# Order of TensorE's work in an attention round: value products, scores and both heads' transposes in one stretch, then the up products

## The chip, the cores and the metric

One core of one Trainium2 chip runs the kernel. The metric is the device time of one execution, in microseconds (us). A core has five engines with a queue of instructions each, executed in order: TensorE (PE in the profile; its weight loads are the row PEld), VectorE (DVE), ScalarE (ACT), GpSimd (POOL) and SyncE (SP), which here only issues DMAs. TensorE writes to PSUM, of which there are eight banks of 512 fp32 columns; ScalarE and VectorE read them.

## The reference

The kernel computes three parts one after the other (shortened; B=2, H=8, S=576, D=64; 1152 tokens, width 512, hidden width 1536):

```python
# 1: attention with a memory term, causal
a = softmax(mask(q @ k.T / 8))              # per batch and head
local = a @ v
q_p = where(q > 0, q, exp(q) - 1) + 1
mem = (q_p @ M_prev) / (q_p . z_prev + 1e-6)
x = g * mem + (1 - g) * local               # g = sigmoid(beta), heads side by side: [1152, 512]
# 2: gated MLP
gt, val = x @ w_gate, x @ w_val             # the "up" products
x = (gt * sigmoid(gt) * val) @ w_out
# 3: top-1 mixture of 8 experts with a capacity
e = argmax(x @ w_gate2); x = prob[e] * (relu(x[kept] @ w1[e]) @ w2[e])
```

## The kernel before, in words

All products are fp32 in effect. The up products split each operand into a high and a low part (xh, xl; wh, wl) and add three products, so that TensorE can take them in its faster fp32 form; scores, transposes and value products are plain fp32.

**Attention** is cut into 40 units. A group is a batch b, a half e of the sequence (rows 0 to 255, or 256 to 575) and a pair p of heads; it has two or three units, one for each block of up to 128 query rows. `first[n]` is the first unit of group n. For a unit u these functions emit the work:

- `emit_s` (L195): the scores of both heads into one PSUM tile `s` (two buffers), and the mask. `emit_max` (L215): VectorE's negated row maxima, scaled. `emit_exp` (L224): ScalarE's exponential from `s` into `P`, with row sums; two instructions, one a head, or one for the short last block.
- `emit_norm` (L230): VectorE adds 1e-9 to the sums and inverts them, GpSimd scales `P`.
- `emit_t(u, x)` (L238): transposes of head x of `P` on TensorE into a PSUM bank `tp`, and a copy to `PT`, which in all units is ScalarE's.
- `emit_av` (L264): value products from `PT` into the PSUM tile `u` (one buffer). In a group's last unit it adds the memory term, and ScalarE and VectorE write the group's result as `xh` (L287) and `xl` (L288). The next group's first value products need `u` back, so they wait for `xl`.

**The phi chores** prepare q_p for the memory term, for each batch and each of five row blocks: `phi_load`, `phi_exp` (ScalarE), `phi_sum` (VectorE, then GpSimd), `phi_norm` (VectorE, then GpSimd's division, L157 to L162), `phi_t` (L164: four transposes into a PSUM bank `tphi`, and ScalarE's copy to `ph`). They and the loads are laid on **ticks** by a table of constants `T` (L299 to L316): `at_tick(t, ...)` puts a chore on tick t, `do(t)` runs tick t's chores.

**The order** is written out by hand: the whole kernel stands under a manual schedule, so each engine executes its instructions in the order in which the Python code emits them. The generator `attn` (L318) runs rounds k = -3 to 40 of three ticks each. In round k the scores of unit k+3 are computed (LA = 3), the normalization of unit k+2 and the exponential of k+3, the transposes of k and the value products of k-1. After each tick it yields, and the driving loop (L537) may then take a **piece** from the generator `up` (L428): six up products, half of one result in a PSUM bank `gv`. Two pieces fill a bank. With the first piece of a bank `up` emits the evaluation of the bank before (tanh on ScalarE, L459, and VectorE's products L460 and L465), and with every piece a share of the preparation of the next weights: ScalarE's copies wh (L405), VectorE's or GpSimd's differences wl (L408), VectorE's unpacking of the raw weights (L374 to L379), and loads and stores of weights. The number of pieces by a tick is `cnt * total // (tb - ta)`: none before tick 35 (round 11), then 28 pieces up to tick 65 and 68 from there to the end, so three or four a round.

`gv`, `tp` and `tphi` share three PSUM banks (L83). A bank is given out again when all that reads it is done.

After attention, `up(2)` (L623) does the second batch's up products with the preparation of w_out; then come the down products with the routing, and the experts.

Of the kernel before, what the change touches and what calls it, by code (L numbers as in the profile page):

```python
# [36 lines left out]
T = dict(LA=3, lv0=-7, lv1=-21, le=-21, sc=-17, lp=-2, sk0=0, sk1=1, sq0=-5, sl0=-2, sq1=-6, sl1=-4, pl=-20,  # L37
         pe=0, ps=2, pn=4, pt=9, k00=-3, k01=-1, k02=1, k03=4, k04=8, kb0=-2, kb1=-4, kb2=4, kb3=2,
         kb4=8, lb=-11, n0=2, ns=9, RW=3, RS=2, ev0=1, ev1=1, ev2=1, lo0=8, lo1=24, sp0=-9, ka=8,
         kb=2, kc=0, w0=-15, w1=-3, rb=1, ob=2, vb=5, qb=5, Pb=4, xb=4, kk=0, xf=7, sx=2, t00=5, t01=1,  # L40
         t02=5, t03=8, t04=0, tb0=3, tb1=0, tb2=4, tb3=-1, tb4=-1, pre=1, rk=[8, 10], gt=[6, 7, 10,
         11], xr=7)
# [3 lines left out]
def tile_attention_moe(  # L46
# [36 lines left out]
    def bank(name):  # L83
        return psb.tile([128, 512], F32, tag="m", bufs=3, name=name)
# [12 lines left out]
    def cols(n):  # L97

        e = groups[n][1]
        return (HALF, S - HALF, S) if e else (0, HALF, HALF)  # L100
# [79 lines left out]
    NU = len(units)  # L180
# [14 lines left out]
    def emit_s(u):  # L195
        n, i = units[u]
        o, m = QT[i]
        w = o + m
        s = psa.tile([128, 2, 512], F32, tag="s", bufs=2, name="s")
        s_t[u] = s  # L200
        heads = [op_t[n][64 * h:64 * h + 64] for h in range(2)]
        if i < 4:
            for h, t in enumerate(heads):
                nc.tensor.matmul(s[:, h, 0:w], lhsT=t[:, 0, o:w], rhs=t[:, 1, 0:w], start=True, stop=False)  # L204
            for h in range(2):
                nc.tensor.matmul(s[:, h, o:w], lhsT=identb, rhs=maskb, start=False, stop=True)  # L206
        else:
            c = S // 2
            for a in range(2):
                for h, t in enumerate(heads):  # L210
                    nc.tensor.matmul(s[64 * h:64 * h + 64, a, 0:c], lhsT=t[:, 0, o:w], rhs=t[:, 1, a * c:a * c + c],
                                     start=True, stop=(a == 0), skip_group_check=True)
            nc.tensor.matmul(s[:, 1, c - 64:c], lhsT=identb, rhs=maskb2, start=False, stop=True, skip_group_check=True)

    def emit_max(u):  # L215
        P = at.tile([128, 2, 512], F32, tag="P", bufs=T["Pb"], name="P")
        st = at.tile([128, 3, 2], F32, tag="st", bufs=5, name="st")
        sv, vs = views(u, s_t[u], P)
        k = len(vs)
        nc.vector.tensor_reduce(out=st[:, 0, 0:k], in_=sv, axis=AX.X if k == 2 else AX.XY, op=ALU.max, negate=True)  # L220
        nc.vector.tensor_scalar(st[:, 0, 0:k], st[:, 0, 0:k], 0.125, None, op0=ALU.mult)  # L221
        p_t[u] = (P, st, vs)

    def emit_exp(u):  # L224
        P, st, vs = p_t[u]
        for x, (a, c, gm) in enumerate(vs):
            nc.scalar.activation(c, a, AF.Exp, bias=st[:, 0, x:x + 1], scale=0.125, accum_out=st[:, 1, x:x + 1])  # L227
        s_t.pop(u)

    def emit_norm(u):  # L230
        P, st, vs = p_t[u]
        k = len(vs)
        nc.vector.tensor_scalar(st[:, 1, 0:k], st[:, 1, 0:k], 1e-9, None, op0=ALU.add)
        nc.vector.reciprocal(st[:, 2, 0:k], st[:, 1, 0:k])  # L234
        for x, (a, c, gm) in enumerate(vs):
            nc.gpsimd.tensor_scalar(c, c, st[:, 2, x:x + 1], gm, op0=ALU.mult, op1=ALU.mult)  # L236

    def emit_t(u, x):  # L238

        n, i = units[u]  # L240
        P = p_t[u][0]
        if x == 0:
            pt_t[u] = at.tile([128, 2, 512], F32, tag="PT", bufs=2, name="PT")
        PT = pt_t[u]
        t = bank("tp")
        mode = T["ev" + str(0 if u < first[NP] else 1 if u < first[2 * NP] else 2)]
        ev = (nc.scalar.copy, nc.vector.tensor_copy)[(x % 2, 0, 1, x % 2 * (u % 2))[mode]]
        tv = t.rearrange("p (j m) -> p j m", m=128)
        if i < 4:
            for j in range(i + 1):  # L250
                nc.tensor.transpose(out=tv[:, j, :], in_=P[:, x, j * 128:(j + 1) * 128], identity=ident)  # L251
            ev(PT[:, x, 0:128 * (i + 1)], t[:, 0:128 * (i + 1)])  # L252
        else:
            pf, ptf = (z.rearrange("p a b -> p (a b)") for z in (P, PT))
            for y, j in enumerate(((0, 1, 2), (3, 4))[x]):
                kw = QT[j][1]
                nc.tensor.transpose(out=tv[0:kw, y, :], in_=pf[:, j * 128:j * 128 + kw], identity=ident)
            if x == 0:
                ev(ptf[:, 0:384], t[:, 0:384])
            else:  # L260
                ev(ptf[:, 384:512], t[:, 0:128])
                ev(ptf[0:64, 512:640], t[0:64, 128:256])

    def emit_av(u):  # L264
        n, i = units[u]
        vt = v_t[n]
        o, m = QT[i]
        PT = pt_t.pop(u)
        p_t.pop(u)
        ptf = PT.rearrange("p a b -> p (a b)")  # L270
        g0, gw, _ = cols(n)
        if u == first[n]:
            u_t[n] = psb.tile([128, 512], F32, tag="u", bufs=1, name="u")
        U = u_t[n]
        c0 = o - g0
        for j in range(i + 1):
            kw = QT[j][1]
            for h in range(2):
                rhs = PT[:, h, j * m:j * m + m] if i < 4 else ptf[0:kw, j * 128 + 64 * h:j * 128 + 64 * h + 64]
                nc.tensor.matmul(U[64 * h:64 * h + 64, c0:c0 + m], lhsT=vt[0:kw, j, 64 * h:64 * h + 64],  # L280
                                 rhs=rhs, start=(j == 0 and u == first[n]), stop=False, skip_group_check=True)
        if u + 1 == NU or units[u + 1][0] != n:
            b, e, p = groups[n]
            zt, mt, ph = batch_t[b]
            U, gs = u_t.pop(n)[:, 0:gw], slice(g0, g0 + gw)
            nc.tensor.matmul(U, lhsT=mt[:, p, :], rhs=ph[e][:, p, :], start=False, stop=True, skip_group_check=True)
            nc.scalar.copy(xh[b][:, p, gs], U)  # L287
            nc.vector.tensor_sub(xl[b][:, p, gs], U, xh[b][:, p, gs].bitcast(F32))  # L288
# [3 lines left out]
    def at_tick(t, fn, *args):  # L292
        chores.setdefault(t, []).append((fn, args))

    def do(t):
        for fn, args in chores.pop(t, ()):
            fn(*args)

    for n, (b, e, p) in enumerate(groups):  # L299
        k = 3 * (first[n] - LA)  # L300
# [4 lines left out]
    for b in range(B):  # L305
        k = first[2 * NP * b]
        for i in range(5):
            t = 3 * (k + T["k%s%d" % ("0b"[b], i)])
            if b or i > 1:
                at_tick(t + T["pl"], phi_load, b, i)  # L310
            at_tick(t + T["pe"], phi_exp, b, i)
            at_tick(t + T["ps"], phi_sum, b, i)
            at_tick(t + T["pn"], phi_norm, b, i)
            at_tick(t + T["pt"] + T["t%s%d" % ("0b"[b], i)], phi_t, b, i)
        if b:
            at_tick(3 * k + T["lb"], load_batch, b)  # L316

    def attn():  # L318
        for t in range(min(chores), -3 * LA):
            do(t)  # L320
        for k in range(-LA, NU + 1):
            do(3 * k)
            if k + LA < NU:
                emit_s(k + LA)
                emit_max(k + LA)
            if 0 <= k < NU:
                emit_t(k, 0)
            yield 3 * k
            do(3 * k + 1)
            if 0 <= k + LA - 1 < NU:  # L330
                emit_norm(k + LA - 1)
            if k + LA < NU:
                emit_exp(k + LA)
            if 0 <= k < NU:
                emit_t(k, 1)
            yield 3 * k + 1
            do(3 * k + 2)
            if 0 <= k - 1:
                emit_av(k - 1)
            yield 3 * k + 2  # L340


# [194 lines left out]
    for t in attn():  # L537
        if t < t0:
            continue
        if gi == 0 and t >= t1:  # L540
            for _ in gens[0][0]:
                pass
            gi, cnt, done = 1, 0, 0
        cnt += 1
        gen, ta, tb, total = gens[gi]
        while done < cnt * total // (tb - ta):
            next(gen, None)
            done += 1
# [613 lines left out]
```

## Time and profile before

| | |
|---|---|
| time, median of 3 runs | 562.18 us (559.9 to 564.96) |
| profiled execution | 562.79 us, span 561.0 us |
| mean granted TensorE clock | 0.983 |
| busy: PE, PEld, DVE, ACT, POOL | 94%, 77%, 66%, 49%, 38% of the span |
| attention and first up products | from the start to about 225 us |
| second batch's up products | about 225 to 305 us |

The busy shares are averages over stages with different limits. A busy TensorE is not TensorE at its peak: products are pipelined, so the distance from start to start is a better measure of their cost than the duration of one. Rows of a timeline give start, duration, engine, line, operation, operands and count, and in brackets the idle time of the engine just before it and what ended it. PEclk is the granted clock as a share of full speed; a stretch without a record of it is shown as 1.00.

### The profile page before, as it was taken

What the parts mean: (1) busy time and instruction counts of PE and PEld (TensorE: products, weight loads), DVE (VectorE), ACT (ScalarE), POOL (GpSimd) and SP (SyncE); (2) the same over time, 40 slices, a digit from 0 to 9 for tenths busy, and PEclk for the clock granted to TensorE, in tenths of its full rate; (3) what the DMA queues carried; (4) which work ended last, traced back from release to release, by engine and by line L of the source; (5) the groups of instructions that cost most, each with busy time, mean ns of one, the idle gap of its engine ahead of it and who ended that gap; (6) DMA issues with size and microseconds to landing.
All of it is one profiled execution on the core that took longest, in us unless ns stands there. A gap on an engine that the chain in (4) does not pass through costs nothing. (4 is left out here: it accounts for less than half of the span.)

```text
span 561.0 us, 9629 instructions
## 1 busy us (share of the span) xinstructions
PE 525.5 (94%) x3433; PEld 431.2 (77%) x3433; DVE 370.3 (66%) x788; ACT 272.3 (49%) x603; POOL 213.8 (38%) x259
## 2 busy tenths in 40 slices
PE   4789997999989999999999999999978999999996
PEld 2446776887767789999999887778766978888774
DVE  6778888557786541678877487975867681728080
ACT  4467665466644452233353234434767562726171
POOL 4767647547264331222223475863223111020220
PEclk9998998899989999999999999998999999999999
DMA  8568384326552110599981335354789855464430
GB/s 274 199 218 255 107 288 136 95 69 256 172 142 84 39 39 1 175 271 277 275 263 32 120 87 215 94 184 161 245 299 305 294 201 186 132 240 158 168 105 8
DMA packets 43005, 96.33 MB, mean 172 GB/s; under 512 B 4598, under 2 KB 15350, under 8 KB 41408
## 3 DMA queue, kind: packets, MB, share of 16 engines
q1 hardware_dynamic: 41184, 91.04, 50.3%
q0 software_dynamic: 1760, 4.50, 2.1%
q8 instruction: 36, 0.59, 0.4%
q14 instruction: 25, 0.20, 0.1%
HBM read 78.68 MB, written 17.72 MB: 172 GB/s over the span
## 5 line engine op out<-in xcount | busy, mean ns | idle before, releaser
L444 PE MATMUL gv<-xh,wh 128*128 128x256 f32 (+1 forms) x384 | 123.2, 321 | 4.1 <-ACT PT L252 1.9
L444 PE MATMUL gv<-xh,wl 128*128 128x256 f32 (+1 forms) x384 | 114.7, 299 | 1.2 <-POOL wl L408 1.1
L444 PE MATMUL gv<-xl,wh 128*128 128x256 f32 (+1 forms) x384 | 114.0, 297 | 0.0
L236 POOL TENSOR_SCALAR P<-P,st,omg 128x128 f32<-128x128 f32 (+4 forms) x72 | 65.3, 915 | 66.7 <-DVE st L234 38.5
L444 PEld LDWEIGHTS gv<-xh,wh 128*128 128x128 f32 x384 | 73.3, 191 | 8.9 <-issue 3.6
L444 PEld LDWEIGHTS gv<-xh,wl 128*128 128x128 f32 x384 | 73.3, 191 | 2.2 <-POOL wl L408 2.1
L444 PEld LDWEIGHTS gv<-xl,wh 128*128 128x128 f32 x384 | 73.5, 191 | 0.7
L1030 POOL DMA_INDIRECT out_dram<-hT,gi x13 | 15.6, 1197 | 124.5 <-ACT hT L1029 101.7
L408 POOL TENSOR_TENSOR wl<-wf,wh 128x512 fp32r<-128x512 f32 x27 | 39.7, 1471 | 59.6 <-ACT wh L405 56.0
L227 ACT ACTIVATE P<-s,st 128x128 f32<-128x128 f32 (+4 forms) x72 | 39.1, 549 | 31.9 <-DVE st L221 22.7
L220 DVE TENSOR_REDUCE st<-s 128x2 f32<-128x256 f32 (+4 forms) x40 | 32.2, 805 | 21.4 <-PE s L206 17.0
L818 PE MATMUL y<-wo_h,hh 128*128 128x512 f32 x108 | 43.3, 401 | 0.0
L252 ACT COPY PT<-tp 128x128 f32<-128x128 f32 (+3 forms) x64 | 27.2, 426 | 33.0 <-PE tp L251 32.9
L679 DVE SCALAR_TENSOR_TENSOR prod<-y,wrb 128x512 f32<-128x512 f32 x56 | 34.8, 686 | 11.9 <-ACT xr L676 11.9
L818 PE MATMUL y<-wo_h,hl 128*128 128x512 f32 x108 | 42.4, 392 | 0.0
L818 PE MATMUL y<-wo_l,hh 128*128 128x512 f32 x108 | 42.4, 392 | 0.0
L405 ACT CAST wh<-wf 128x512 fp32r<-128x512 f32 x54 | 33.7, 624 | 14.3 <-DMA wf<-wsp 14.3
L460 DVE SCALAR_TENSOR_TENSOR th<-th,gv 128x256 f32<-128x256 f32 (+1 forms) x48 | 21.6, 451 | 27.0 <-ACT th L459 26.9
L280 PE MATMUL u<-PT,vt 128*64 128x128 f32 (+1 forms) x480 | 34.7, 279 | 4.1 <-DVE xl L288 4.1
L204 PE MATMUL s<-qk 64*128 64x128 f32 (+3 forms) x128 | 30.1, 553 | 6.8 <-DMA qk<-in_qk_dram 4.1
L1010 DVE SCALAR_TENSOR_TENSOR hcl<-w,hch 128x288 fp32r<-128x288 f32 x24 | 10.9, 456 | 35.1 <-ACT hch L1009 35.0
L280 PEld LDWEIGHTS u<-PT,vt 128*64 128x64 f32 x480 | 24.4, 143 | 12.1 <-issue 4.9
(372 smaller groups left out, 1250.2 us busy)
## 6 DMA issues: line engine op xcount, KB each, us to landing
hT<-in_w_dram SPq DMA_DIRECT2D x64, 512.0 KB, 5.4
wr<-in_wgv_dram SPq DMA_DIRECT2D x12, 1024.0 KB, 5.9
wf<-wsp SPq DMA_DIRECT2D x15, 512.0 KB, 5.0
wor<-in_w_out_dram SPq DMA_DIRECT2D x12, 512.0 KB, 4.6
wsp<-wf SPq DMA_DIRECT2D x10, 512.0 KB, 6.8
disp<-pad SPq DMA_DIRECT2D x16, 257.0 KB, 7.0
xd<-disp SPq DMA_DIRECT2D x14, 257.0 KB, 7.3
qk<-in_qk_dram SPq DMA_DIRECT2D x8, 320.0 KB, 4.2
```

What stands on the lines that cost most here:

```text
L204: nc.tensor.matmul(s[:, h, 0:w], lhsT=t[:, 0, o:w], rhs=t[:, 1, 0:w], start=True, stop=False)
L220: nc.vector.tensor_reduce(out=st[:, 0, 0:k], in_=sv, axis=AX.X if k == 2 else AX.XY, op=ALU.max, negate=True)
L227: nc.scalar.activation(c, a, AF.Exp, bias=st[:, 0, x:x + 1], scale=0.125, accum_out=st[:, 1, x:x + 1])
L236: nc.gpsimd.tensor_scalar(c, c, st[:, 2, x:x + 1], gm, op0=ALU.mult, op1=ALU.mult)
L252: ev(PT[:, x, 0:128 * (i + 1)], t[:, 0:128 * (i + 1)])
L280: nc.tensor.matmul(U[64 * h:64 * h + 64, c0:c0 + m], lhsT=vt[0:kw, j, 64 * h:64 * h + 64], rhs=rhs, start=(j == 0 and u == first[n]), stop ...
L405: nc.scalar.copy(hi[:, sl], w[:, sl])
L408: (nc.gpsimd if pool_ else nc.vector).tensor_sub(lo[:, sl], w[:, sl], hi[:, sl].bitcast(F32))
L444: nc.tensor.matmul(a, lhsT=wt[:, s, c, :], rhs=xt[b][:, c, sl], start=(c == 0 and y == 0), stop=(c == KC - 1 and y == 2))
L460: nc.vector.scalar_tensor_tensor(out=th[:, 0:w], in0=th[:, 0:w], scalar=1.0, in1=a, op0=ALU.add, op1=ALU.mult)
L679: nc.vector.scalar_tensor_tensor(out=prod[e % 2], in0=y, scalar=1.0, in1=wrb[e], op0=ALU.mult, op1=ALU.mult, accum_out=lg[:, e:e + 1])
L818: nc.tensor.matmul(y, lhsT=a[:, k, :], rhs=w[:, k, :], start=st, stop=en)
```

## The change

Within a round the value products of unit k-1 move from the end to the front, the second head's transposes of unit k come directly behind the first head's, and normalization and exponential follow; only then come the round's three places for up products, with the chores of the ticks 3k+1 and 3k+2 still between them. The ticks of `phi_t` are rounded down to a multiple of three, so that its transposes are emitted at a round's start. For batch 0 they go from 5, 7, 17, 29, 33 to 3, 6, 15, 27, 33, for batch 1 from 66, 57, 85, 74, 92 to 66, 57, 84, 72, 90 (blocks 0 to 4). Nothing else is changed.

```diff
-            at_tick(t + T["pt"] + T["t%s%d" % ("0b"[b], i)], phi_t, b, i)
+            at_tick((t + T["pt"] + T["t%s%d" % ("0b"[b], i)]) // 3 * 3, phi_t, b, i)
...
         for k in range(-LA, NU + 1):
             do(3 * k)
+            if 0 <= k - 1:
+                emit_av(k - 1)
             if k + LA < NU:
                 emit_s(k + LA)
                 emit_max(k + LA)
             if 0 <= k < NU:
                 emit_t(k, 0)
-            yield 3 * k
-            do(3 * k + 1)
+                emit_t(k, 1)
             if 0 <= k + LA - 1 < NU:
                 emit_norm(k + LA - 1)
             if k + LA < NU:
                 emit_exp(k + LA)
-            if 0 <= k < NU:
-                emit_t(k, 1)
+            yield 3 * k
+            do(3 * k + 1)
             yield 3 * k + 1
             do(3 * k + 2)
-            if 0 <= k - 1:
-                emit_av(k - 1)
             yield 3 * k + 2
```

## Rows read from the trace of the kernel before

**Rows 1.** Busy time of each engine by stage; stretch, length, then busy (instructions), clock, DMA.
```profile
4.00:59.00 55.00, 45.90 (x282) 26.39 (x282) 43.06 (x102) 33.26 (x104) 36.30 (x37) 0.97 0.73 243
59.00:96.00 37.00, 33.85 (x300) 26.82 (x298) 33.01 (x61) 22.62 (x61) 23.17 (x16) 0.98 0.52 173
...
96.00:102.00 6.00, 6.00 (x38) 4.95 (x37) 1.75 (x5) 2.17 (x6) 3.39 (x4) 0.55 0.59 173
...
160.00:167.00 7.00, 5.10 (x29) 3.48 (x28) 6.83 (x14) 3.69 (x10) 3.98 (x4) 0.76 0.22 40
...
59.00:225.00 166.00, 159.71 (x1304) 129.07 (x1303) 108.17 (x227) 85.52 (x234) 76.22 (x72) 0.97 0.36 118
```

**Rows 2.** Timeline of TensorE, round 15.
```profile
75.04 0.36 PE L444 MATMUL gv<-xh,wh 128*128 128x256 f32 x1
75.24 0.28 PE L444 MATMUL gv<-xl,wh 128*128 128x256 f32 x1
75.36 0.29 PE L444 MATMUL gv<-xh,wl 128*128 128x256 f32 x1
...
75.84 0.60 PE L251 MATMUL tp<-ident,P 128*128 128x128 f32 x4
76.19 0.36 PE L444 MATMUL gv<-xh,wh 128*128 128x256 f32 x1
...
77.08 0.88 PE L280 MATMUL u<-PT,vt 128*64 128x128 f32 x12
77.88 0.39 PE L444 MATMUL gv<-xh,wh 128*128 128x256 f32 x1
...
78.79 0.46 PE L211 MATMUL s<-qk 64*64 64x288 f32 x2
```

**Rows 3.** Timeline of TensorE, a round without up products.
```profile
48.31 1.04 PE L251 MATMUL tp<-ident,P 128*128 128x128 f32 x8
49.19 0.60 PE L172 MATMUL tphi<-ident,px 128*128 128x128 f32 x4
```

**Rows 4.** Timeline of TensorE's weight loads, round 15.
```profile
75.24 0.19 PEld L444 LDWEIGHTS gv<-xh,wl 128*128 128x128 f32 x1
...
77.08 0.63 PEld L280 LDWEIGHTS u<-PT,vt 128*64 128x64 f32 x12
```

**Rows 5.** Timelines of ScalarE and TensorE at two waits for a copy.
```profile
84.47 0.26 ACT L262 COPY PT<-tp 64x128 f32<-64x128 f32 x1
...
84.78 0.39 PE L444 MATMUL gv<-xh,wh 128*128 128x256 f32 x1 [0.29 <-ACT PT L262]
...
160.03 0.69 ACT L227 ACTIVATE P<-s,st 128x512 f32<-128x512 f32 x1 [3.19 <-DVE st L221]
...
162.01 0.39 PE L444 MATMUL gv<-xh,wh 128*128 128x256 f32 x1 [1.90 <-ACT PT L252]
```

**Rows 6.** Timelines of VectorE and GpSimd, division for one phi block, round 23.
```profile
121.53 0.68 DVE L157 TENSOR_REDUCE nm<-pe 128x8 f32<-128x512 f32 x1
...
123.00 1.04 POOL L162 TENSOR_TENSOR px<-px,nm 128x512 f32<-128x512 f32 x1 [2.46 <-DVE st L233]
```

**Rows 7.** Groups of ScalarE by shape, 0 to 225 us: busy us, mean ns, idle before.
```profile
L252 ACT COPY PT<-tp 128x512 f32<-128x512 f32 x16 | 9.4, 586 | 8.5 <-PE tp L251 8.5
...
L252 ACT COPY PT<-tp 128x256 f32<-128x256 f32 x16 | 6.0, 373 | 7.8 <-PE tp L251 7.8
```

**Rows 8.** TensorE's waits before 59 us (total, times, longest); timeline of ScalarE.
```profile
PE u L280 <- DVE xl L288: 4.1, 2, 2.3
...
39.90 0.69 ACT L227 ACTIVATE P<-s,st 128x512 f32<-128x512 f32 x1 [2.68 <-DVE st L233]
...
41.39 0.39 ACT L287 CAST xh<-u 128x256 fp32r<-128x256 f32 x1
```

**Rows 9.** TensorE before 59 us: four transposes; busy time, clock and DMA.
```profile
24.68 1.06 PE L251 MATMUL tp<-ident,P 128*128 128x128 f32 x4
...
47.00:59.00 12.00, 11.95 (x110) 1.00 0.67 221
```

## The prediction

> **What bounds the kernel now.** I read the busy time by stage first. From 59 to 225 us, where attention and up products share the engines, TensorE is busy 159.71 of 166 us [rows 1]; no other engine comes near over the whole stage. From 59 to 96 us VectorE has 33.01 of 37 us of work, and TensorE still idles there [rows 1]. Before 59 us attention runs alone: TensorE 45.90 of 55 us, VectorE 43.06 [rows 1]. After 225 us the other batch's up products keep TensorE busy, so what TensorE loses or saves before 225 us moves the end. The second view is TensorE's timeline of one round [rows 2]: what is to be seen is the start-to-start distance of the up products, 0.12 us inside a piece, and how long six of them hold the engine when attention stands before and behind. The third is who kept TensorE waiting [rows 5, 8].
>
> **Seams.** A piece is six up products, 6 x 0.12 = 0.72 us by their distance [rows 2]. The three pieces of this round take 75.04 to 75.84, 76.19 to 77.08 and 77.88 to 78.79: 0.80, 0.89 and 0.91 us, 0.44 us over 3 x 0.72 [rows 2]. About 0.08 is the entry, 0.09 the exit to value products or scores; the exit to transposes is free. One stretch keeps one entry and one exit, 0.17, and saves 0.27. Against it, four transposes take 0.35 us from their start to the up product's (75.84 to 76.19), while eight in a row take 0.88 [rows 2, 3]: 0.09 more for the first head. Net 0.18 us in each of the 28 rounds 12 to 39, 5.0 us. Where VectorE is nearly full, up to 96 us, a quicker TensorE only waits for it; I don't count those six rounds: 22 x 0.18 = **-4.0**; ends 0 and -5.0.
> The trace shows where a seam lies: inside a piece the weights of the product that starts at 75.36 are loaded from 75.24, one distance ahead, but the first weights of the value products are loaded at 77.08, when they start [rows 2, 4]. The Trainium skill, TensorE: Matmul & The Clock Gate, "Architectural detail", says that the engine's queue can pull a weight load ahead of products in flight; taken without exception this makes seams free, and the sum would be 3 to 4 us higher. The trace agrees inside a piece and disagrees at the seam.
>
> **Banks.** Transposes and up products share three PSUM banks. A bank holds two pieces, and its reading is issued only behind the next bank's first piece. Counting pieces by the tick formula, 15 rounds begin with a bank that is full and not yet read; both heads' transposes now take the other two, so the next up product waits for the first head's copy by ScalarE. Where a copy was waited for, the up product followed its end (84.47 + 0.26) by 0.05 us, after 0.29 us of idle [rows 5]. The copy is 0.37 us for 256 columns and 0.59 for 512 [rows 7], and the second head's transposes (0.35) run beside it. I take the 0.29 of the row, in the 12 of these rounds behind 96 us: **+3.5**. Ends 0 (ScalarE is early) and 15 x 0.6 = 9 (a further copy ahead on its queue).
>
> **Phi transposes.** Their ticks are rounded down to the round's start. All keep four or more ticks behind the division except two of batch 1 (74 to 72, 92 to 90), which then stand two ticks behind it. From the first VectorE operation to the end of GpSimd's product takes 121.53 to 124.04, 2.5 us [rows 6]; between them now lie three pieces, at least 2.2 us, and the whole next stretch is queued behind on TensorE. **+0.5** for both; ends 0 and 5 (GpSimd also has the scaling of P, which the change puts ahead).
>
> **Waits of before.** At 162.01 an up product waited 1.90 us for a PT copy, which stood on ScalarE behind an exponential that waited 3.19 us for VectorE's maximum [rows 5]; the granted clock of 160 to 167 us is 0.76 [rows 1], 7 x 0.24 = 1.7 us. Now both copies come ahead of that exponential. But VectorE's lateness stays, and can turn up at the next transposes. Ends 0 and -3.6; I take **-2.0**.
>
> **Rounds without up products.** In rounds 0 to 11 the value products formerly came a whole round behind their transposes. Now they follow directly, and nothing covers the second head's copy, 0.37 to 0.59 and 0.05 behind it, say 0.55 us. Of 12 such places, 5 hold phi transposes in between: 7 x 0.55 = +3.9. The copies also stand behind the exponential of the round before, which in one case waited 2.68 us for VectorE's queue [rows 8]; at most four rounds x 2.68 = 10.7, at least 0; I take +1.5. The gain: twice, 4.1 us together, value products wait for xl of the pair before, because the copy xh at 41.39 stood behind that exponential at 39.90 [rows 8]; xh now comes a stretch earlier on ScalarE. I take 4.0 of it. Together **+1.4**; ends -0.2 and +14.6.
>
> Nothing is computed more or less. SP's queue keeps its order, as loads and weight copies stay at their ticks and pieces; they start earlier or later with the pieces, and none is on the path here. On GpSimd the scaling of P goes ahead of one piece's weight split; between a step's last weight split and its use there still lie two pieces and a stretch, so I cost that at nothing; without the stretch as cover it would be one 1.3 us split at a step's start.
>
> **Sum.** -4.0 + 3.5 + 0.5 - 2.0 + 1.4 = -0.6 us. The profiled execution took 562.8 us (span 561.0 and 1.8 around it), so 562.2; it lay 0.6 above the median, 562.2, of the three runs, so 561.6 us against that median.
>
> **Rivals.**
> *Slower, the hand-over of PT.* In rounds 0 to 11 the ring transposes, copy, value products, scores becomes the bound. For: VectorE has 43.06 of 55 us of work there and ScalarE waited up to 2.68 us for it [rows 1, 8], and one round less lies between copy and use. Against: TensorE itself is busy most of that time, and scores still run three units ahead. With half of its worst price and no gain from xl or the old waits: -4.0 + 3.5 + 0.5 + 3.9 + 5.4 = +9.3, about 571 us; in full 577. It decides over 1% from about 8 us of new waits. The same gaps can keep the clock low: four transposes took 1.06 us at 24.68 and 0.60 at 75.84 [rows 2, 9], 1.77 times, the engine at its lower level (1.2 GHz) early on, though no record shows it there, and although idle only in short gaps; it came to the higher level in an unbroken stretch. Should 47 to 59 us (11.95 us busy, clock 1.00) stay low, 9.2 us more: 580 to 586. Chance 0.25, of it 0.05 with the clock.
> [...]
>
> *Faster, the waits fall too.* All 28 seams (5.0), the old wait with its clock (3.6), the xl waits (4.1), no bank waits, less 3.9 of hand-over: -8.8, 553 us. If TensorE's 3.15 us of idle time from 59 to 96 us and the clock of 0.55 from 96 to 102 us (2.7 us) [rows 1] also go, 548. For: ScalarE's long waits before were exponentials blocking copies, and the change puts copies first. Against: VectorE's queue, which made them late, is not shorter. Chance 0.28.
>
> *It does not do what it says.* Seams vanish on paper only, because the ticks' other work puts waits between the pieces; then nothing moves, 562. No TensorE work is left in those ticks, so 0.02.
>
> **How the numbers follow.** My forecast, gains and new waits of like size, has 0.45. Predicted 561.6 us. Within 1% (5.6 us, about what a measurement here can tell from no change) lie it and the last rival: 0.47; faster 0.28; slower 0.25. The range, 553 to 571, reaches to the middle of both rivals and leaves about 0.2 outside (the far halves of both); the forecast's own is 557 to 567.
>
> **What would show it.** Seams: one piece's first product 0.12 behind the last piece's, three or four pieces in a row, and one entry and one exit per round. Banks: waits of up products for PT copies of the first head, some 0.3 us in about every second round; if they are absent, faster is nearer. Hand-over: waits of value products for PT before 59 us, 4 to 6 us in total; over 8, slower. The xl waits gone or not, and the phi transposes of rounds 24 and 30 waiting for px or not. The start of the first up product tells the part without up products from the rest. The forecast is wrong if that start moves by over 4 us, if the clock falls in the stretches, or if VectorE's maxima come later and ScalarE blocks the copies after all.

## The result and the profile after

| | before | after |
|---|---|---|
| median (10 runs each) | 560.66 us (558.99 to 564.96) | 568.52 us (566.15 to 574.39) |
| profiled execution, its span | 562.79, 561.0 us | 569.03, 567.3 us |
| start of up(2) | 226.45 us | 234.09 us |

The ratio is 1.0141 [1.0112, 1.017]: the change costs 7.9 us by the medians and 6.3 by the two profiled spans. The time lies in the range, but the likeliest case was "within 1%"; the slower case had 0.25, and for another reason than the one that acted.

Both orders do the same up products, so the same piece marks the same point of the work. The last piece of round 12 starts at 61.79 us before and 61.84 after; the start of up(2) differs by 7.63 us, the down products' by 6.37. The loss lies between round 12 and up(2). First the busy times over the work from round 12 to up(2), which is the same in both kernels, after (stretch, length, then busy of PE, PEld, DVE, ACT, POOL with instructions, clock, DMA):

```profile
61.84:234.09 172.25, 157.08 (x1286) 125.67 (x1284) 107.34 (x224) 85.21 (x231) 74.50 (x75) 0.98 0.36 118
```

The same view of before, the same work:

```profile
61.79:226.45 164.66, 158.37 (x1285) 128.04 (x1284) 106.74 (x226) 84.34 (x231) 77.30 (x75) 0.97 0.37 119
```

TensorE's busy time fell by 1.29 us (158.37 to 157.08), its idle time rose from 6.29 to 15.17: +8.88 - 1.29 = 7.6 us, the whole loss. The mean granted clock over this work is 0.97 before and 0.98 after, so the loss is not the clock's. What it waited for, after, 59 to 240 us (total, times, longest):

```profile
PE tphi L172 <- POOL px L162: 3.5, 2, 3.1
PE tp L251 <- DVE hT L465: 3.1, 2, 2.3
PE gv L444 <- ACT PT L252: 2.7, 10, 0.3
PE tp L251 <- ACT PT L252: 2.6, 1, 2.6
PE gv L444 <- ACT PT L259: 1.1, 3, 0.4
PE gv L444 <- POOL wl L408: 0.7, 1, 0.7
PE tphi L172 <- DVE th L460: 0.6, 1, 0.6
PE tp L251 <- DVE th L460: 0.5, 1, 0.5
...
```

The same view of before, 59 to 226 us:

```profile
PE gv L444 <- ACT PT L252: 1.9, 1, 1.9
PE gv L444 <- DVE hT L465: 1.1, 1, 1.1
PE gv L444 <- POOL wl L408: 1.0, 2, 0.7
PE tp L251 <- POOL px L162: 0.9, 1, 0.9
PE tp L251 <- ACT ph L173: 0.7, 1, 0.7
PE gv L444 <- ACT PT L262: 0.3, 1, 0.3
```

Read the right-hand names as banks. `gv`, `tp` or `tphi` that waits for `PT`, `th` or `hT` wants one of the three PSUM banks, and the name is that of the read that gives it back. After, these are 3.1 + 2.7 + 2.6 + 1.1 + 0.6 + 0.5 = 10.6 us; before 1.1 + 0.3, and the long 1.9. Two kinds are to be told apart. In the first a round begins with a full, unread bank: the two heads' transposes take the other two, and the up product waits for the first head's copy (13 times, 2.7 + 1.1 us). TensorE's timeline, after, round 14:

```profile
71.68 0.39 PE L444 MATMUL gv<-xh,wh 128*128 128x256 f32 x1 [0.29 <-ACT PT L252]
...
72.38 0.28 PE L444 MATMUL gv<-xh,wl 128*128 128x256 f32 x1
72.50 0.28 PE L444 MATMUL gv<-xh,wh 128*128 128x256 f32 x1
```

0.29 us is the very row from which it was priced [rows 5]. From 72.38 to 72.50 one piece ends and the next begins, 0.12 us as inside a piece: the seam of [rows 2] is gone. The second kind was not foreseen: a round begins with a half-filled bank, and the bank before it, whose evaluation was issued only behind that half, is not yet free. Then the first head's transposes take the last bank and the second head's find none. This happens in rounds 15, 18 and 29 (3.1 + 2.6 + 0.5 us). In round 18 (96.11) the bank that came free was that of the first head's copy, which ScalarE made only at 95.40, behind the two activations of a phi block; the evaluation came later still, at 95.87. The 0.6 us of `tphi` fall in round 28, which begins with a full bank and has the phi transposes as one more user. All engines, after, at the two longest waits of 150 to 180 us:

```profile
159.19 1.22 DVE L379 SCALAR_TENSOR_TENSOR wf<-wr,wf 128x1024 int32<-128x1024 int32 x1
159.34 2.19 POOL L408 TENSOR_TENSOR wl<-wf,wh 128x512 fp32r<-128x512 f32 x1 [1.01 <-ACT wh L405]
...
159.61 0.61 PE L251 MATMUL tp<-ident,P 128*128 128x128 f32 x4
...
160.32 1.75 DVE L150 SCALAR_TENSOR_TENSOR px<-pe,px 64x512 f32<-64x512 f32 x1
...
162.00 0.47 DVE L465 SCALAR_TENSOR_TENSOR hT<-th,gv 128x320 f32<-128x320 f32 x1
...
162.53 0.66 PE L251 MATMUL tp<-ident,P 128*128 128x128 f32 x4 [2.31 <-DVE hT L465]
...
168.99 1.03 POOL L162 TENSOR_TENSOR px<-px,nm 64x512 f32<-64x512 f32 x1 [0.59 <-DVE nm L160]
169.16 3.17 DVE L379 SCALAR_TENSOR_TENSOR wf<-wr,wf 128x1024 int32<-128x1024 int32 x1
169.99 1.26 POOL L408 TENSOR_TENSOR wl<-wf,wh 128x512 fp32r<-128x512 f32 x1
170.08 0.46 PE L172 MATMUL tphi<-ident,px 64*128 64x64 f32 x4 [3.12 <-POOL px L162]
```

The evaluation's product (162.00) stands on VectorE behind an unpacking (159.19) and a phi sum (160.32); 0.06 us after its end the second head's transposes start, 2.31 us late. TensorE's waits before 59 us, after, and the timeline at the second of them:

```profile
PE tphi L172 <- POOL px L162: 3.4, 2, 2.8
PE u L280 <- issue: 2.1, 1, 2.1
PE u L280 <- ACT PT L252: 1.4, 4, 0.6
...
37.47 0.41 DVE L288 TENSOR_TENSOR xl<-u,xh 128x256 fp32r<-128x256 f32 x1
...
37.98 0.60 PE L280 MATMUL u<-PT,vt 128*64 128x128 f32 x4 [2.14 <-issue]
```

Of the two waits for xl, 4.1 us before [rows 8], one is left. The list calls it issue, but the value products at 37.98 are the first of a group, which need `u` back, and they start 0.10 us behind the end of xl (37.88). The waits for `px` and for the copies are new.

### The profile page after: what moved, and what is told of

The parts are those of the page before. It is cut to its first block, busy times and chain, and to the rows that moved or that the text cites. A ratio compares the mean times of both kernels' runs of the same rounds, so it can differ in the third digit from the quotient of the medians.

```text
span 567.3 us, 9640 instructions
## 1 busy us (share of the span) xinstructions
PE 523.1 (92%) x3433; PEld 427.9 (75%) x3433; DVE 368.8 (65%) x788; ACT 273.9 (48%) x603; POOL 209.3 (37%) x259
## 5 line engine op out<-in xcount | busy, mean ns | idle before, releaser
L444 PE MATMUL gv<-xh,wh 128*128 128x256 f32 (+1 forms) x384 | 117.0, 305 | 3.8 <-ACT PT L252 2.7
L236 POOL TENSOR_SCALAR P<-P,st,omg 128x128 f32<-128x128 f32 (+4 forms) x72 | 57.1, 800 | 89.9 <-DVE st L234 76.2
L408 POOL TENSOR_TENSOR wl<-wf,wh 128x512 fp32r<-128x512 f32 x27 | 41.3, 1529 | 60.3 <-ACT wh L405 54.0
L252 ACT COPY PT<-tp 128x128 f32<-128x128 f32 (+3 forms) x64 | 24.6, 430 | 34.0 <-PE tp L251 34.0
L280 PE MATMUL u<-PT,vt 128*64 128x128 f32 (+1 forms) x480 | 36.2, 275 | 4.0 <-issue 2.1
L204 PE MATMUL s<-qk 64*128 64x128 f32 (+3 forms) x128 | 28.5, 527 | 6.7 <-DMA qk<-in_qk_dram 4.2
```

The costliest lines, as they stand in the source:

```text
L408: (nc.gpsimd if pool_ else nc.vector).tensor_sub(lo[:, sl], w[:, sl], hi[:, sl].bitcast(F32))
L444: nc.tensor.matmul(a, lhsT=wt[:, s, c, :], rhs=xt[b][:, c, sl], start=(c == 0 and y == 0), stop=(c == KC - 1 and y == 2))
```

## The experiments

The expectations name theories: **P**, phi transposes too close behind their division; **Q**, the two heads' transposes in one stretch lack a bank, because the evaluation of `gv` comes late; **R**, the hand-over from copy to value products in the rounds without up products; **S**, VectorE's full queue is what lengthens every wait; **T**, an earlier evaluation helps any order; **U**, the long stretch itself. Ratios stand against the kernel before, run beside each kernel on the same chip; its median there was 562.3 to 562.8 us, above the 560.7 from which the ranges of the first four expectations were set.

**1. The changed kernel with the phi ticks of before** (one tick apart, 7 to 6, which the new order needs).

```diff
-            at_tick((t + T["pt"] + T["t%s%d" % ("0b"[b], i)]) // 3 * 3, phi_t, b, i)
+            at_tick(t + T["pt"] + T["t%s%d" % ("0b"[b], i)] - (b == 0 and i == 1), phi_t, b, i)
```

> The changed kernel with the phi transposes on their old ticks (only batch 0's block 1 goes from tick 7 to 6, since the value products that use it are now at the start of round 2). Kernel before 560.7, changed kernel 568.5. Theory P (phi transposes two ticks behind their division hold TensorE at a round's start): about half of the loss goes, 563 to 565, the 3.1 us wait of round 30 is gone. Theory Q (bank waits): 567 to 569, as the bank waits stay. Theory R (moving the value products is the loss): 567 to 569.

Measured: 571.69 us, 1.0155 [1.011, 1.02], above every range. No better. The px wait is gone from the list after 59 us, but an up product now waits 3.3 us for VectorE's `th`, and up(2) still starts at 232.83. P falls as the cause of half the loss.

**2. The kernel before with the rounded phi ticks.**

```diff
-            at_tick(t + T["pt"] + T["t%s%d" % ("0b"[b], i)], phi_t, b, i)
+            at_tick((t + T["pt"] + T["t%s%d" % ("0b"[b], i)]) // 3 * 3, phi_t, b, i)
```

> The kernel before with nothing but the rounded ticks of the phi transposes. Theory P: 563 to 566, with waits of the phi transposes for px in rounds 24 and 30. Theory Q and theory R: 560 to 561.5.

Measured: 564.03 us, 1.0036 [1.0002, 1.0069]. This lies in P's range, though the kernel before took 562.28 beside it: the ticks cost 1.8 us here and at most 0.7%, so not the 1.4%.

**3. The kernel before with only the value products moved to the front** (and tick 7 to 6).

```diff
             do(3 * k)
+            if 0 <= k - 1:
+                emit_av(k - 1)
...
-            if 0 <= k - 1:
-                emit_av(k - 1)
```

> The kernel before with the value products alone moved to the round's start (phi ticks old but 7 to 6). Theory Q: one seam per round less and hardly a bank wait, 556 to 560. Theory R (nothing covers the copy of PT before 59 us, and the value products delay the scores by one place): 564 to 567. Theory P: 559 to 562.

Measured: 578.79 us, 1.0286 [1.0247, 1.0325]. Round 12's last piece starts 16.6 us later than before (78.37); from there to up(2) 1.1 us come back. No theory had it so slow. TensorE's waits, 4 to 76 us:

```profile
PE u L280 <- ACT PT L252: 15.5, 17, 2.3
```

The second head's copy still stands behind the next exponential on ScalarE, and the value products now need it at once. That is the hand-over rival at full size (577 us in the prediction). In the changed kernel the second head's transposes come before that exponential, and the same wait is 1.4 us.

**4. The kernel before with only the second head's transposes moved up.**

```diff
                 emit_t(k, 0)
+                emit_t(k, 1)
...
-            if 0 <= k < NU:
-                emit_t(k, 1)
```

> The kernel before with the second head's transposes alone moved up behind the first head's, value products at the round's end, old phi ticks. Theory Q: a bank that is full but not yet read at a round's start makes the next up product wait about 0.3 us for a copy in some 10 to 15 rounds, 563 to 565. Theories P and R: 559 to 561.5.

Measured: 563.83 us, 1.0028 [1.0001, 1.0056]. It is 2.0 us ahead in round 12 and 5.1 in round 19 (start of the last piece), and loses all of it again: up(2) starts at 226.88, 0.43 later. Its waits, 59 to 227 us, hold the thirteen waits for a copy of the changed kernel to the tenth:

```profile
PE gv L443 <- ACT PT L252: 2.7, 10, 0.3
PE tp L257 <- DVE hT L464: 1.5, 1, 1.5
...
PE gv L443 <- ACT PT L259: 1.1, 3, 0.4
PE tp L257 <- DVE th L459: 1.0, 1, 1.0
```

So the waits for a copy come with the two transposes in one stretch, whatever the value products do. They are not the whole loss: from round 12 to up(2) this order takes 2.4 us longer than before (167.08 against 164.66), the changed one 7.6. Its bank waits are 7.3 us (1.0 of them not shown), not 10.6, and it has none for `px` there.

**5. The changed kernel with a full bank evaluated at the round's end**, not behind the next bank's first piece.

```diff
-        pend = []
+        pend = full[n]
...
+        if t % 3 == 2 and full[gi]:
+            full[gi].pop()()
```

> The changed kernel; a bank of up products that is full at a round's end is evaluated there, instead of behind the next round's first piece. Kernel before 562.3, changed kernel 568.5. Theory Q (both heads' transposes in one stretch need two of the three banks, so up products and second transposes wait): the waits of up products for a PT copy (3.8 us) and most waits of transposes for VectorE's evaluation (3.6 us) go, 561 to 564. Theory R (the value products' hand-over costs the loss): 567 to 569. Theory S (VectorE is late with its queue, and the stretch meets it wherever the banks are): 566 to 569, with the waits moved to other transposes.

Measured: 562.2 us, 1.0008 [0.9977, 1.004]. The loss is gone; up(2) starts at 224.65, 9.4 us earlier than in the changed kernel. The work from round 12 to up(2), and TensorE's waits, 59 to 225 us:

```profile
60.62:224.65 164.03, 154.47 (x1286) 125.79 (x1284) 106.76 (x224) 84.64 (x231) 75.51 (x75) 0.98 0.38 124
...
PE gv L446 <- DVE th L462: 2.7, 1, 2.7
PE tp L251 <- ACT PT L252: 1.5, 1, 1.5
...
PE gv L446 <- ACT PT L252: 0.8, 3, 0.3
PE gv L446 <- ACT PT L259: 0.4, 1, 0.4
```

The thirteen short waits of up products are four; the bank waits fell from 10.6 to 5.4 us. Q's time holds, though half of its waits are left; 2.6 us of the gain are busy time (157.08 to 154.47), at the same mean clock of 0.98, and their cause is open.

**6. The same evaluation in the kernel of run 4** (diffs of 4 and 5).

> Second head's transposes moved up, value products left at the round's end, phi ticks old, and a full bank evaluated at the round's end. Without that evaluation this order took 563.8. Theory Q: 558 to 560.5, better than the kernel before. Theories R and S: 562.5 to 564.5.

Measured: 559.34 us, 0.9935 [0.9904, 0.9966]: the best of the kernels with all the work, and faster than the kernel before. In its profiled execution, the slowest of the twelve (563.89), it was 5.0 us ahead of before in round 29 and lost 3.5 in round 30.

**7 and 8. Less work for VectorE**, in the changed kernel and in the one before: two of the three operations that unpack each raw weight are left out.

```diff
-        if fresh[c]:
+        if fresh[c] and step == 0:
```

> The changed kernel with two of the three VectorE operations that unpack each of the first product's raw weights left out (about 2.4 us a weight tile; its numbers are then not the reference's). To be set against the kernel before with the same left out. Theory S: the loss against it shrinks to under 3 us. Theory Q: waits for the copies stay, 4 to 6 us. Theory R: 7 to 9 us stay.

> The kernel before with the same two VectorE operations left out. Theory S: 553 to 558, as some of its own waits go too, and the changed order then within 3 us of it. Theories Q and R: 556 to 561, the changed order 4 to 9 us above it.

Measured: 549.37 us, 0.9729 [0.9677, 0.9782], and 538.52 us, 0.9583 [0.9546, 0.9621]. Both gain, the kernel before more than any theory had, and the gap grows from 7.9 to 10.9 us: S falls as the cause of the whole. The changed kernel, light, 56 to 217 us:

```profile
PE gv L444 <- ACT PT L252: 2.7, 10, 0.3
...
PE gv L444 <- ACT PT L259: 1.1, 3, 0.4
```

The kernel before, light, 53 to 209 us:

```profile
PE tphi L172 <- ACT PT L262: 0.5, 1, 0.5
PE tp L251 <- DVE st L233: 0.4, 1, 0.4
```

With VectorE free the old order has hardly a wait left. The new one loses its waits for `th` and `hT` but none of the thirteen for a copy: those are the order's own. Of the 8.3 us between the two at the start of up(2) (216.69 and 208.36) 2.9 are there by round 12, so from round 12 to up(2) the loss is 5.4 us, against 7.6 with the full work. By these profiles VectorE's load adds the other 2.2. Why the medians are 10.9 apart, not 8.3, was not tried.

**9. The evaluation at the round's end in the kernel before** (diff of 5), a control.

> The kernel before with a full bank evaluated at the round's end: the control for the same edit in the changed order, which there gave 6 us back. Theory Q (only a stretch with both heads' transposes needs that bank): 561 to 564, no change from 562.5. Rival T (early evaluation helps any order, and the 6 us say nothing of the stretch): 556 to 559.

Measured: 562.6 us, 0.9999 [0.9968, 1.003]. The earlier evaluation gained in runs 5 and 6, where both heads' transposes stand in one stretch, and nothing here; T falls.

**10. The changed kernel with the value products at the end of the stretch**, behind both heads' transposes.

```diff
             do(3 * k)
-            if 0 <= k - 1:
-                emit_av(k - 1)
...
                 emit_t(k, 1)
+            if 0 <= k - 1:
+                emit_av(k - 1)
```

> The changed kernel with the value products at the end of the stretch, behind both heads' transposes, instead of its front. Theory Q: the value products (0.4 to 1.7 us) now cover the copy that the next up product waits for, so the 3.8 us of those waits go, the waits of the transposes for VectorE's evaluation stay, and the hand-over before 59 us is covered: 560 to 564. Rival U (the length of the stretch itself costs): 567 to 569.

Measured: 563.74 us, 1.0026 [0.9996, 1.0055]. As long a stretch with the same work in it, and nearly the whole loss is gone: U falls. Its timeline in round 14:

```profile
68.70 0.86 ACT L252 COPY PT<-tp 128x384 f32<-128x384 f32 x2 [1.92 <-PE tp L251]
68.87 0.95 PE L280 MATMUL u<-PT,vt 128*64 128x64 f32 x20
...
70.15 0.52 PE L444 MATMUL gv<-xh,wh 128*128 128x256 f32 x1
```

The copies (68.70) run under the value products (68.87), and the up product finds its bank free. Of the thirteen waits for a copy none is left in this trace; the waits of transposes for a late evaluation stay, 59 to 227 us:

```profile
PE tp L251 <- DVE hT L465: 3.4, 2, 2.5
PE tp L251 <- ACT PT L252: 2.4, 1, 2.4
PE tphi L172 <- POOL px L162: 1.0, 1, 1.0
...
```

With 1.8 us of such waits that are not shown, the bank waits are 7.6 us, 3.0 less than in the changed kernel. Another 2.5 of the gain stand at `px` (3.5 to 1.0), so this run is not a test of the banks alone.

**11. The same with the evaluation at the round's end** (diffs of 5 and 10).

> The same with a full bank evaluated at the round's end. Theory Q: no bank waits and one seam pair a round, 556 to 559. Rival U: 561 to 564.

Measured: 564.2 us, 1.0019 [0.9983, 1.0054]: a miss for Q, no gain on top, and just above the range that U gave. The profile shows a place: it is 3.9 us ahead of before in round 29 and 0.7 behind in round 30. Its longest wait, 59 to 240 us:

```profile
PE tphi L172 <- POOL px L162: 3.1, 1, 3.1
```

It ends at 163.30 and is for the division of the last phi block, two ticks ahead of its transposes. Whether this alone ate the gain was not tried.

**12. The old order up to round 11, the changed one from round 12 on.**

```diff
-            if 0 <= k - 1:
+            if first[NP] + 4 <= k:
                 emit_av(k - 1)
...
+            old = k < first[NP] + 4
+            if old:
+                yield 3 * k
+                do(3 * k + 1)
...
+            if old and 0 <= k - 1:
+                emit_av(k - 1)
```

> The order of before in rounds below 12 (no up products there) and the changed order from round 12 on, phi ticks as in the changed kernel. Theory Q: the loss lies behind 59 us, 566.5 to 569. Theory R (the hand-over of PT in the rounds without up products): 561 to 564.

Measured: 571.04 us, 1.0174 [1.0129, 1.0219], above both ranges. The whole loss is there with the old order before 59 us: R falls.

## Why the prediction was wrong

| step | predicted | profiled execution |
|---|---|---|
| Seams | -4.0 | -1.3 (busy time) |
| Banks | +3.5 | +9.2 (10.6 against 1.4) |
| Phi transposes | +0.5 | +1.9 (3.5 against 0.9 + 0.7) |
| Waits of before | -2.0 | -1.9 |
| Rounds without up products | +1.4 | +0.05 |
| split on GpSimd | 0 | -0.1 (0.9 against 1.0) |
| up(2) | 0 | -1.3 |

The right column adds up to 6.55, rounded as it is; the spans differ by 6.3.

**Banks is the step that failed most, by 5.7 us; Seams was mis-sized by 2.7.** The mechanism of Banks was right and half of its size too: up products wait 0.3 us for the first head's copy in 13 rounds, 3.8 us against 3.5. That these agree is in part luck: three of the 13 waits lie before 96 us, where the prediction counted none, and its 12 rounds behind 96 us come out of the tick formula only with round 40, which has no transposes. What was missed is the other parity. The count took the rounds that begin with a full, unread bank and left out those that begin with a half-filled one, where the transposes themselves run out of banks: 6.2 us, and 0.6 at the phi transposes. The upper end, 9, was about there, but it came from a further copy on ScalarE, not from a late evaluation. Runs 5 and 10 each take the loss away from a different side (free the bank earlier; cover the copy), run 4 shows the waits for a copy without the rest of the change, and run 9 that the earlier evaluation is worth nothing in the old order. That the bank waits are the loss is shown by run 5 best, with half of them left; what each kind takes of the medians' 7.9 us was not measured apart.

The Trainium skill, Perfetto Trace Analysis, "Matmuls", says that independent groups should rotate through banks so that the reading of one overlaps the next one's products. The trace agrees: the change packs four users of a rotation of three into one stretch, and TensorE waited 10.6 us for a bank.

**Waits of before** went as feared in its own last sentence: the 1.90 us wait [rows 5] is gone, and the next transposes wait 2.31 us in about the same place, on VectorE's evaluation. The step was right and its gain was booked again under Banks.

**Seams** were priced from one kind of round. Behind 96 us eight rounds have no wait in either kernel (from the start of one round's last piece to that of the next). Four of them (25, 33, 38, 39) are 0.17 us shorter on average, as priced with 0.18. The other four (20, 22, 34, 37) are 0.09 longer: each begins a new group, so its value products are the last of the group before and end in the memory term (L286), and behind that now stand the scores, not an up product. Round 20, before and then after:

```profile
108.66 0.81 PE L286 MATMUL u<-ph,mt 128*128 128x320 f32 x2
109.06 0.52 PE L444 MATMUL gv<-xh,wh 128*128 128x256 f32 x1
...
106.66 0.81 PE L286 MATMUL u<-ph,mt 128*128 128x320 f32 x2
107.40 0.70 PE L204 MATMUL s<-qk 64*128 64x256 f32 x4
```

From its start to the next product are 0.40 us before, 0.74 after. Of the 22 rounds that were counted, 8 begin a group; 14 at -0.17 and 8 at +0.09 make -1.7, near the -1.3 of the busy time.

**Phi transposes** showed more than was priced, 3.12 us in round 30. By run 1 nothing is gained where this wait is taken away: a wait for VectorE of the same size stands in its place. By run 2 the ticks alone cost 1.8 us, at most 0.7%.

**Rounds without up products** came out even, but not by the prediction's steps. Of the xl gain of 4.0 only 2.0 arrived, the hand-over was 1.4 us instead of 3.9 + 1.5, and px (3.4) came in, which was not foreseen there. The rival built on this place had the right sign for the wrong reason; run 3 shows the size that it has where the copy stays behind the exponential. Its case of a low clock did not come: 47 to 59 us ran at 1.00 again.

## What to carry to other kernels

When one engine's work is gathered into a longer stretch, count what the stretch keeps alive at once, half-filled buffers included, against the buffers of the rotation, for every phase that a round can begin in. Then either free the full buffer before the stretch begins (run 5), or put independent work behind the producers, where it covers their copies (run 10). A wait in the list is worth its length only if nothing late stands behind it: run 1 removed the 3.5 us for `px` and gained nothing.

## What the runs showed of the hardware

Some operations of VectorE and GpSimd kept each other waiting for whole instructions. The median of L379's twelve is 1.22 us, but it took 3.17 at 169.16, where it began while the first of two GpSimd products ran and ended about one own duration after the second (169.99 + 1.26 = 171.25, + 1.22 = 172.47 against 172.33). At 160.32 L150 took 1.75 instead of 0.68 us beside the split of 159.34, which itself took 2.19 instead of 1.27 because L379 had started first. That is how the evaluation at 162.00 came so late. The Trainium skill, SBUF — State Buffer, "SBUF: two separate sides", describes an exclusive lock that the first comer holds for its whole instruction, for an operation of VectorE with two SBUF inputs against one of GpSimd that reads SBUF. The trace agrees in these rows: L379 reads wr and wf, L150 pe and px, and they took 3.17 and 1.75 us.
